# The second MLP product of five quads of token tiles as seven half-size products

## The chip, the cores and the metric

One NeuronCore of a Trainium2 chip runs the kernel in one launch. The metric is the device time in microseconds, smaller is better. Engines are named as in the profile: PE is TensorE (PEld its weight loads), DVE VectorE, ACT ScalarE, POOL GpSimd, SP SyncE, which here only starts transfers.

## The reference, cut to what matters

The inputs are float32: q, k, v of 4 batches, 8 heads, 768 tokens, 64 wide; the model width is 512, the hidden width 2048.

```python
scores = q @ k^T / 8, masked by blocks of 32        # per batch and head
x   = softmax(scores) @ v                            # -> batch, 768 tokens, 512
a1  = alpha1 * x + beta1
u   = x + lam * einsum('ts,bsd->btd', w_tok, a1)     # product over tokens
a2  = alpha2 * u + beta2
out = u + lam * (relu(a2 @ w_ch1) @ w_ch2)           # the MLP, per token
```

The change is in the last product, hidden (768 x 2048) times w_ch2 (2048 x 512), of two of the four batches. The kernel multiplies the columns of w_ch2 by lam beforehand (`w2b`).

## The kernel before

Heads go in pairs, 16 pairs in all, four to a batch. `emit_qk` (L582) makes the scores of a unit on TensorE, `emit_exp` (L600) their exponentials on ScalarE into an `eT` tile, `emit_keep` (L617) multiplies them by a mask on VectorE, and `emit_pv_keys` (L652) multiplies by v into the PSUM tile `op`, of which there is one. `emit_finish` (L669, L670) divides by the row sums into `x_sb`, and so frees `op` for the next head. `emit_a1pp` (L686, L687, mostly on POOL) makes a1. When two pairs are done, `job_tok2` (L826) makes the product over tokens for them in three groups; each is added to `x_sb` on VectorE (L838, an eviction) and cast to bf16 into `ubf` (`emit_cast`, L844).

The MLP needs u transposed. `emit_udma` (L868) lets a transposing DMA of the SP queue do this, and `emit_uscale` (L877) applies alpha2 and beta2. `job_ut` (L853, L854) does the same on TensorE and VectorE; it serves pairs 2 and 3 only. `job_f1(b, c, n)` (L891, L898) makes 128 hidden channels of 384 tokens: four matmuls of 384 columns and a ReLU on ScalarE into `hts`. There are 32 such jobs to a batch. `job_f2(b, o, g)` (L910) makes a quarter of the second product of a tile of 128 tokens: four matmuls of 512 columns, sixteen in all to a tile, in one PSUM bank; after the last, VectorE adds x (L919) into `ot`, which SP stores. The last tile of all goes in two column parts, 384 and 128 wide (`job_f2_cols`, L930, L938).

PSUM has eight banks: two `sp` tiles of two banks for the scores, three `mm` banks that go round, and one `op`.

The order is written by hand. The first five pairs run under a plan; the other eleven follow strings in which one letter is one job, in program order: q three units of scores, x an exponential, k a mask, p a pv job, f a `job_f1`, g a quarter of `job_f2`, T a third of `job_tok2`, d and v the DMA and the scaling of u, digits what the plan has for that time. `W1` takes nine rows to the end of batch 0's heads and beyond, `W2` twelve rows of three units, one batch, and runs twice (batch 2's and batch 3's heads, with the MLP of the batch before); `W3` is the last stage, the token product and MLP of batch 3:

```python
WEAVE = W1 + W2 * (B - 2) + W3
```

Every engine works through its own queue in that order; Tile's semaphores make an instruction wait for what it reads, and for the readers of what it overwrites. So an instruction that waits holds up all that stand behind it on its engine.

Of the kernel before, what the change touches and what calls it, by code (L numbers as in the profile page):

```python
# [25 lines left out]
DM = 512  # L26
P = 128
NT = S // P
NH = 4 * DM // P
QC = 384  # L30
NP = H // 2
# [11 lines left out]
W1 = [  # L43
# [9 lines left out]
]  # L53
W2 = [
# [12 lines left out]
]  # L67
W3 = [
# [3 lines left out]
]  # L72
WEAVE = W1 + W2 * (B - 2) + W3
ENG = {
    "kT0": 0,
    "kT1": 0,
# [153 lines left out]
def kernel(  # L230
# [16 lines left out]
    nc = tc.nc  # L247
# [22 lines left out]
    ap_ = ctx.enter_context(tc.tile_pool(name="attn", bufs=1))  # L270
# [4 lines left out]
    def ptile(shape, dt, name):  # L275
        return pp.tile(shape, dt, name=name, tag=name)
# [36 lines left out]
    qk0 = ap_.tile([P, 2, NT, 2, D], BF, name="qk", tag="qk", bufs=1)  # L313
# [9 lines left out]
    qTs = [ptile([P, 2, S], BF, f"qTs{i}") for i in range(NQB // 2)]  # L323
    kTs = [ptile([P, 2, S], BF, f"kTs{i}") for i in range(NQB // 2)]
# [24 lines left out]
    for n, src in enumerate((moe_lam, moe_alpha1, moe_beta1)):  # L349
# [10 lines left out]
        out=identb[:],  # L360
        in_=identb[:],
# [32 lines left out]
    for o in (slice(0, 4), slice(4, NT)):  # L394
# [47 lines left out]
    def sp_tile():  # L442
        return psum.tile([P, 2, 512], FP, name="sp", tag="sp", bufs=2)
# [111 lines left out]
    x_sbs = {}  # L555
# [137 lines left out]
    al2T, be2T = ab2T[:, 0:4], ab2T[:, 4:8]  # L693
# [97 lines left out]
    ubfs = {}  # L791
# [49 lines left out]

    def emit_cast(i, sl):
        b, hp = i // NP, i % NP
        nc.vector.tensor_copy(out=ubfs[i][:, sl, :], in_=x_sbs[b][:, sl, ts(hp, P)])  # L844

    def job_ut(i, half=None):
        b, hp = i // NP, i % NP
        if hp == 0:
            uTs[b] = ap_.tile([P, 4, S], BF, name="uT", tag="uT", bufs=2)
        sl = slice(0, NT) if half is None else slice(3 * half, 3 * half + 3)  # L850
        tps = mm_tile((P, NT, P), BF)
        for o in range(NT)[sl]:
            nc.tensor.transpose(tps[:, o, :], ubfs[i][:, o, :], identb[:])  # L853
        nc.vector.tensor_scalar(  # L854
            out=uTs[b][:, hp, :].rearrange("p (o t) -> p o t", o=NT)[:, sl, :],
            in0=tps[:, sl, :],
            scalar1=al2T[:, hp : hp + 1],
            scalar2=be2T[:, hp : hp + 1],
            op0=ALU.mult,
            op1=ALU.add,  # L860
        )


    uraws = {}
# [8 lines left out]
    def emit_uscale(i):  # L873
        b, hp = i // NP, i % NP
        if hp == 0:
            uTs[b] = ap_.tile([P, 4, S], BF, name="uT", tag="uT", bufs=2)
        nc.vector.tensor_scalar(  # L877
            out=uTs[b][:, hp, :],
            in0=uraws.pop(i)[:],
            scalar1=al2T[:, hp : hp + 1],  # L880
            scalar2=be2T[:, hp : hp + 1],
            op0=ALU.mult,
            op1=ALU.add,
        )

    def job_f1(b, c, n):
        if n == 0:
            hts[(b, c)] = ap_.tile([P, NH, QC], BF, name="hts", tag="hts", bufs=2)
        ps = mm_tile()
        for dk in range(4):  # L890
            nc.tensor.matmul(  # L891
                ps[:, 0:QC],
                w1b[:, dk, ts(n, P)],
                uTs[b][:, dk, ts(c, QC)],
                start=(dk == 0),
                stop=(dk == 3),
            )
        nc.scalar.activation(  # L898
            hts[(b, c)][:, n, :], ps[:, 0:QC], AF.Relu
        )  # L900

    chs = {}

    def job_f2(b, o, g):
        if g == 0:
            chs[(b, o)] = mm_tile()
        ps = chs[(b, o)]
        ht = hts[(b, o // 3)]
        for nk in range(4 * g, 4 * g + 4):
            nc.tensor.matmul(  # L910
                ps[:],
                ht[:, nk, ts(o % 3, P)],
                w2b[:, nk, :],
                start=(nk == 0),
                stop=(nk == NH - 1),
            )
        if g == 3:
            ot = ap_.tile([P, DM], FP, name="ot", tag="ot", bufs=3)
            nc.vector.tensor_tensor(  # L919
                out=ot[:], in0=x_sbs[b][:, o, :], in1=ps[:], op=ALU.add  # L920
            )
            nc.sync.dma_start(
                out[b].rearrange("(p o) n -> p o n", o=NT)[:, o, :], ot[:]
            )

    def job_f2_cols(b, o, sl):
        ps = mm_tile()
        ht = hts[(b, o // 3)]
        for nk in range(NH):
            nc.tensor.matmul(  # L930
                ps[:, sl],
                ht[:, nk, ts(o % 3, P)],
                w2b[:, nk, sl],
                start=(nk == 0),
                stop=(nk == NH - 1),
            )
        ot = ap_.tile([P, DM], FP, name="ot", tag="ot", bufs=3)
        nc.vector.tensor_tensor(  # L938
            out=ot[:, sl], in0=x_sbs[b][:, o, sl], in1=ps[:, sl], op=ALU.add
        )  # L940
        nc.sync.dma_start(
            out[b].rearrange("(p o) n -> p o n", o=NT)[:, o, sl], ot[:, sl]
        )

    NPAIR = B * NP
    WIDE = [
# [28 lines left out]
    ]  # L975
    N1 = MP * len(WIDE)
    LAG = 2
    todo = {"f": [], "g": [], "t": []}

    def start_mlp(b):  # L980
        todo["f"] += [
            lambda c=c, n=n: job_f1(b, c, n) for c in range(2) for n in range(NH)
        ]
        os_ = range(NT) if b < B - 1 else range(NT - 1)
        todo["g"] += [lambda o=o, g=g: job_f2(b, o, g) for o in os_ for g in range(4)]

    def start_pair(i):
        if i % 2 == 0:
# [152 lines left out]
    def token(t, p):  # L1141
        if t == "p":
            pv_next()
        elif t == "k":
            if kept:
                emit_keep(kept.pop(0))
        elif t in "012":
            fns(3 * p + int(t), False)
            fns(3 * p + int(t), True)
        elif t == "L":  # L1150
            if p // 3 + 2 < NPAIR:
                emit_load(p // 3 + 2)
        elif t in "QKY":
            if p // 3 + 1 < NPAIR:
                if t == "Y":
                    emit_lay(p // 3 + 1, "v")
                else:
                    emit_tdma(p // 3 + 1, t.lower())
        elif t == "q":
            for u in range(3 * p, 3 * p + 3):  # L1160
                emit_qk(u)
            exps.extend(range(3 * p, 3 * p + 3))
            exp_next()
        elif t == "x":
            exp_next()
        elif t == "s" and late:
            start_pair(late.pop(0))
        elif t == "T":
            todo["t"].pop(0)()
        elif todo.get(t):  # L1170
            todo[t].pop(0)()

    for p, text in enumerate(WEAVE):
        for t in text.replace(" ", ""):
            token(t, N1 // 3 + p)
    assert not (todo["f"] or todo["g"] or todo["t"] or pend or kept)
    for sl in (slice(0, 3 * P), slice(3 * P, DM)):
        job_f2_cols(B - 1, NT - 1, sl)
# [1 line left out]
_INS = ['q', 'k', 'v', 'sampled_blocks', 'moe_alpha1', 'moe_beta1', 'moe_w_tok', 'moe_alpha2', 'moe_beta2', 'moe_w_ch1', 'moe_w_ch2', 'moe_lam']  # L1180
_OUTS = [((4, 768, 512), 'float32')]
# [25 lines left out]
```

## Time and profile before

| | |
|---|---|
| timed runs | 302.43, 302.67, 302.77 us, median 302.67 |
| span of the profiled execution | 300.1 us (its own time is its span and some 2.6 us around it, by the median) |
| busy TensorE, VectorE, ScalarE, POOL | 293.2, 195.6, 212.7, 112.0 us |
| granted TensorE clock | 1.000 |
| start of batch 3's L891 stage | 255.49 us |
| end of TensorE's work | 297.07 us |

In the profile L12 is line 12 of the kernel, `out<-in` the tiles, and a figure such as 128x512 partitions by elements. Rows of the chain give start, length and what. Rows of the timeline give start, length from the first start to the last end, engine, line and operation, with the idle time before in brackets and who ended it. Rows of groups give the count, the busy time and the mean length of one. A matmul's own length is longer than its share of a stream, since they overlap in the array; so paces are taken from the chain.

### The profile page before, as it was taken

To read this page: it belongs to the slowest core of one execution; us is meant where nothing else is said; L and a number is where in the kernel's file an instruction comes from. 1 tells how busy PE (TensorE), PEld (TensorE's weight loads), DVE (VectorE), ACT (ScalarE), POOL (GpSimd) and SP (SyncE) were. 2 spreads that over 40 slices of the span, in tenths; PEclk is the share of its full clock that TensorE was granted. 3 is DMA by queue.
4 is the path that set the end of the run, shared out by engine and by line. 5 is a ranking of instruction groups with operands and counts; after the bars stand their busy time and mean duration, and the time that the engine had idled before them with its cause. 6 is when DMAs were issued, how large, how long until landed. Compare 5 with 4: busy or idle time off the path is not lost.

```text
span 300.1 us, 7192 instructions
## 1 busy us (share of the span) xinstructions
PE 293.2 (98%) x2970; PEld 183.2 (61%) x2995; DVE 195.6 (65%) x374; ACT 212.7 (71%) x314; POOL 112.0 (37%) x151
## 2 busy tenths in 40 slices
PE   7999999999999999999999999999999999999996
PEld 2788888664577565555675565565576564555543
DVE  4979899985688796963669687972769672000012
ACT  5999999998899944998878763998779400673210
POOL 8997887632525700564315320362322200000000
PEclk9999999999999999999999999999999999999999
DMA  6999999951491993629835693629102004000011
GB/s 182 187 201 187 189 166 196 194 94 28 101 171 21 142 178 81 131 46 149 127 57 86 110 176 85 120 64 135 49 18 52 37 35 122 37 0 37 35 70 70
DMA packets 57929, 31.26 MB, mean 104 GB/s; under 512 B 37989, under 2 KB 54673, under 8 KB 57897
## 3 DMA queue, kind: packets, MB, share of 16 engines
q0 software_dynamic: 16752, 14.22, 33.1%
q1 hardware_dynamic: 40820, 16.19, 26.3%
q8 instruction: 23, 0.38, 0.5%
q10 hardware_dynamic: 324, 0.40, 0.5%
q14 instruction: 10, 0.07, 0.1%
HBM read 29.75 MB, written 6.29 MB: 120 GB/s over the span
## 4 chain that ended last, share of the span: by engine, by line
PE 94%; ACT 3%; DMA 1%; issue 1%; DVE 0%; ACTq 0%
PE mm L891 28%; PE mm L910 26%; PE sp L582 10%; PE op L652 9%; PE mm L826 8%; PE mm L582 4%; PE mm L802 3%; ACT eT L600 2%; PE op L629 2%; PE mm L629 1%; PE mm L930 1%; DMA ms<-ms_c 1%; PE mm L780 1%; PE mm L492 1%; PE mm L532 0%
## 5 line engine op out<-in xcount | busy, mean ns | idle before, releaser
L600 ACT ACTIVATE eT<-sp,expb 128x1024 f16<-128x1024 f32 x111 | 118.3, 1121 | 1.8 <-PE sp L582 1.1
L891 PE MATMUL mm<-uT,w1b 128*128 128x384 bf16 x512 | 92.6, 326 | 0.1
L898 ACT ACTIVATE hts<-mm 128x384 bf16<-128x384 f32 x128 | 60.9, 500 | 42.1 <-PE mm L891 41.5
L617 DVE TENSOR_TENSOR eT<-eT,mask 128x1024 f16<-128x1024 f16 x99 | 80.2, 840 | 15.9 <-ACT eT L600 15.7
L910 PE MATMUL mm<-w2b,hts 128*128 128x512 bf16 x343 | 84.4, 379 | 1.3 <-issue 0.3
L686 POOL TENSOR_TENSOR a1pp<-x_sb,vbc 128x384 bf16<-128x384 f32 x26 | 29.7, 1141 | 124.2 <-DVE x_sb L670 94.7
L891 PEld LDWEIGHTS <-w1b 128*128 128x128 bf16 x512 | 48.2, 98 | 33.3 <-issue 2.1
L600 ACT ACTIVATE eT<-mm,expb 128x512 f16<-128x512 f32 x66 | 41.8, 685 | 27.2 <-PE mm L582 26.8
L910 PEld LDWEIGHTS <-hts 128*128 128x128 bf16 x368 | 33.7, 98 | 38.4 <-issue 4.7
L919 DVE TENSOR_TENSOR ot<-x_sb,mm 128x512 f32<-128x512 f32 x23 | 15.8, 686 | 49.2 <-PE mm L910 41.8
L652 PEld LDWEIGHTS <-eT 128*128 128x128 f16 x792 | 29.9, 98 | 8.3 <-issue 1.3
L652 PE MATMUL op<-vext,eT 128*128 128x65 f16 x792 | 32.1, 194 | 0.2
L687 POOL TENSOR_TENSOR a1pp<-a1pp,vbc 128x384 bf16<-128x384 bf16 x26 | 27.7, 1065 | 2.1
L582 PE MATMUL sp<-qTs,kTs 88*128 88x512 bf16 (+1 forms) x120 | 26.9, 326 | 1.3 <-ACT kTs L432 0.8
L826 PE MATMUL mm<-a1pp,wtokT 128*128 128x256 bf16 x216 | 25.9, 273 | 0.0
L826 PEld LDWEIGHTS <-wtokT 128*128 128x128 bf16 x216 | 20.6, 98 | 5.5 <-issue 2.5
L582 PE MATMUL sp<-qhT,khT 64*128 64x256 bf16 (+1 forms) x176 | 19.7, 322 | 0.0
L838 DVE TENSOR_TENSOR x_sb<-x_sb,mm 128x512 f32<-128x512 f32 x18 | 12.3, 686 | 10.2 <-PE mm L826 10.1
L582 PEld LDWEIGHTS <-khT 64*128 64x128 bf16 x264 | 10.5, 94 | 12.2 <-issue 8.6
L629 PEld LDWEIGHTS <-eT 128*128 128x128 f16 x360 | 14.9, 97 | 3.8 <-issue 0.3
L670 DVE TENSOR_TENSOR x_sb<-op,rcp 128x384 f32<-128x384 f32 x28 | 15.6, 558 | 1.0
L844 DVE CAST ubf<-x_sb 128x256 bf16<-128x256 f32 (+1 forms) x44 | 13.7, 346 | 0.9
(94 smaller groups left out, 221.8 us busy)
## 6 DMA issues: line engine op xcount, KB each, us to landing
out_dram<-ot SPq DMA_DIRECT2D x23, 256.0 KB
qpad<-in_q_dram POOLq DMA_DIRECT2D x15, 192.0 KB, 4.8
kr<-in_k_dram POOLq DMA_DIRECT2D x15, 192.0 KB, 5.5
vr<-in_v_dram POOLq DMA_DIRECT2D x15, 192.0 KB, 6.1
w1b<-in_moe_w_ch_dram POOLq DMA_DIRECT2D x4, 512.0 KB, 9.1
w2b<-in_moe_w_ch_dram POOLq DMA_DIRECT2D x4, 512.0 KB, 8.1
hts<-in_moe_w_tok_dram POOLq DMA_DIRECT2D x2, 576.0 KB, 9.7
x_sb<-in_k_dram ACTq DMA_DIRECT2D x2, 192.0 KB
```

Source lines behind the costliest of these rows:

```text
L582: nc.tensor.matmul(sp[jj][:, dst], lhsT, rhs, start=True, stop=True, skip_group_check=True,)
L600: nc.scalar.activation(dst, at, AF.Exp, bias=expb[:], scale=SCALE)
L617: nc.vector.tensor_mul(out=e, in0=e, in1=keep)
L629: nc.tensor.matmul(op[0][:, o, :], ets[u][:, jj, h * QB + n * P : h * QB + n * P + P], vexts[i % NVB][:, w, 2 * jp + jj, :], start=op[1] == 0,
L652: nc.tensor.matmul(op[0][:, o, :], ets[u][:, jj, h * QB + n * P : h * QB + n * P + P], vexts[i % NVB][:, w, 2 * jp + jj, :], start=op[1] == 0,
L686: eng.tensor_tensor(out=dst, in0=x_sbs[b][:, :, cols], in1=bc[0], op=ALU.mult)
L687: eng.tensor_tensor(out=dst, in0=dst, in1=bc[1], op=ALU.add)
L826: nc.tensor.matmul(ps[:, o], wtokT[:, os_, ts(2 * n + o, P)], a1pps[i][:, os_, :], start=(os_ == 0 and o == 0), stop=(os_ == NT - 1 and o ...
L891: nc.tensor.matmul(ps[:, 0:QC], w1b[:, dk, ts(n, P)], uTs[b][:, dk, ts(c, QC)], start=(dk == 0), stop=(dk == 3),)
L898: nc.scalar.activation(hts[(b, c)][:, n, :], ps[:, 0:QC], AF.Relu)
L910: nc.tensor.matmul(ps[:], ht[:, nk, ts(o % 3, P)], w2b[:, nk, :], start=(nk == 0), stop=(nk == NH - 1),)
L919: nc.vector.tensor_tensor(out=ot[:], in0=x_sbs[b][:, o, :], in1=ps[:], op=ALU.add)
```

## The change

A quad is two tiles of tokens, t and t + 3, with the hidden channels in two halves and the output columns in two halves: a 2 x 2 block product, eight half products before. Now seven, in the form of Strassen's scheme with fewest sums. With A11, A12 (tile t, first and second half of the channels), A21, A22 (tile t + 3) and the quarters B11 to B22 of `w2b`:

- weight sums, once for all quads, sixteen VectorE jobs (`job_t`, letter A, L972 of the changed kernel): T1 = B12 - B11, T2 = B22 - T1, T4 = B21 - T2, T3 = B22 - B12; they lie in tiles that earlier stages leave free, and a new small one
- activation sums, four to a quad (`job_s`, letter S, L1018): X1 = A21 + A22, X2 = X1 - A11, A21 becomes A11 - A21, A12 becomes A12 - X2
- products of eight matmuls of 256 columns each (`mul`, `job_p`, letter g): 1 = A11 B11, 2 = A12 B21, 3 = (A12 - X2) B22, 4 = A22 T4, 5 = X1 T1, 6 = X2 T2, 7 = (A11 - A21) T3
- running sums in PSUM and, after each product, an addition of the 256 or 2 x 256 columns to `x_sb` on VectorE (`plus`, L1054); the output is stored from `x_sb`, and `ot` is gone.

Batch 2 has tiles 1, 4 and 2, 5 as quads (tiles 0 and 3 stay whole), batch 3 all three. In batch 2 product 1 lies in an `mm` bank, product 2 is added to the same half bank, and 6 starts another; in batch 3 product 1 has an `sp` bank, to which 6 and 5 are added, and product 2 an `mm` bank of its own. The last product 3 of all goes in two parts of 128 columns.

The second `W2` becomes `W2L`, with the sixteen A spread over its first nine rows, two f earlier and the first three S at its end; `W3` is new. In batch 3 the f jobs take the channel halves by turns, so that S jobs on half the rows can go between them. The casts and scalings of batch 3's last u go to ScalarE, and of the last two, one is turned by TensorE (letter U, `job_ut`) and one by the DMA.

In program order, around the first products of batch 2: scores of three units, a mask, product 1 of the first quad, a mask, an f job, product 2, an f job, a mask, 24 L652, product 1 of the second quad, scores, product 2 of it, where VectorE has three activation sums of the first quad ahead of the next masks.

```diff
 W2L = [
+    "q 0 p p A g k x L x p f A k 1 K 2 k",
+    "q Q 0 A g x g f v v s T T x A k 1 k p p g g T g g Y d 2 k",
+    "q A g 0 k g d 1 2 p x A k g x k",
+    "q A 0 p k x v Q v 1 2 p k x g k g",
+    "q A 0 p 1 g x A k f K k x f p p k 2 f",
+    "q A k 0 f x f p s f f x 1 L p A k 2 f f f k Y f",
+    "q f L f 0 f A k 1 f Y x f p g x f p f g A k k 2",
+    "q x A k x k Q 0 g 1 s f f g p 2 p f f k p f",
+    "q A T 0 k f 1 x A k f T x f 2 p k K p f",
+    "q x 0 x T k 1 k f 2 k f Q f d p L",
+    "q x 0 x K k g d k s f g f 1 k p p g 2",
+    "q Y x x S S S k g k 0 1 k 2 p g v g v g",
+]
 W3 = [
-    "p p p f g s g T T T g g d d v g g g g g g v g g g f f f f",
-    "f f f f f f f f f f f",
-    "f f f f f f g g f g g f f f f g g g g f g g f f g f g f f g g g g g g g g g g g g",
+    "p p p g s g g T T T S S S d g g U g v S S g g g g g f f f f",
+    "f f f f f f f f f f f f",
+    "f f f f f f f f S S S f f S S S f f S S S f f f f",
+    "S S g S g S g g g S S g S g S g g g S S g S g g g g g S g g g g g",
 ]
-WEAVE = W1 + W2 * (B - 2) + W3
+WEAVE = W1 + W2 + W2L + W3
...
     def emit_cast(i, sl):
-        nc.vector.tensor_copy(out=ubfs[i][:, sl, :], in_=x_sbs[b][:, sl, ts(hp, P)])
+        copy = nc.scalar.copy if i >= NPAIR - 2 else nc.vector.tensor_copy
+        copy(out=ubfs[i][:, sl, :], in_=x_sbs[b][:, sl, ts(hp, P)])
...
+    def affine(i, dst, src):
...
+        if i >= NPAIR - NP:
+            nc.scalar.activation(dst, src, AF.Identity, bias=c, scale=a)
+        else:
+            nc.vector.tensor_scalar(
+                out=dst, in0=src, scalar1=a, scalar2=c, op0=ALU.mult, op1=ALU.add
+            )
...
+    def job_t(dst, a, b, n, k=2):
...
+        nc.vector.tensor_tensor(
+            out=b_rows(dst, n, k),
+            in0=b_rows(a, n, k),
+            in1=b_rows(b, n, k),
+            op=ALU.subtract,
+        )
...
+    def job_s(b, t, n, r=slice(0, HN)):
...
+        nc.vector.tensor_tensor(
+            out=a_of(b, t, dst, r), in0=a_of(b, t, a, r), in1=a_of(b, t, c, r), op=op
+        )
...
+        for r in range(HN):
+            nc.tensor.matmul(
+                ps,
+                a_of(b, t, a)[:, r],
+                b_rows(m, r)[:, 0, cols],
+                start=(start and r == 0),
+                stop=(r == HN - 1),
+                skip_group_check=True,
             )
...
+        if n == 1:
+            mul(b, t, 1, bk[0][:, lo], True)
+            if tail:
+                plus(x[:, t, lo], bk[0][:, lo])
+            else:
+                plus(x[:, t, hi], bk[0][:, lo])
+                plus(
+                    x[:, t + 3].rearrange("p (h c) -> p h c", h=2), twice(bk[0][:, lo])
+                )
+        elif n == 2:
+            ps = bk[1] if tail else bk[0]
+            mul(b, t, 2, ps[:, lo], tail)
...
+    REST = (6, 7, 5, 4, 3)
+    P_ORDER = {
+        2: [(0, g, "g") for g in range(4)]
+        + [(t, n) for t in (1, 2) for n in (1, 2)]
+        + [(3, g, "g") for g in range(4)]
+        + [(t, n) for t in (1, 2) for n in REST],
+        3: [(t, n) for t in range(2) for n in (1, 2)]
+        + [(t, n) for t in range(2) for n in REST]
+        + [(2, n) for n in (1, 2) + REST],
+    }
```

More of the change, by code (lines that the diff above doesn't have):

```diff
@@ L900, in job_f1 @@
         )
+        did.add(("f", b, c, n))
     chs = {}
@@ L917, in job_f2 @@
         if g == 3:
-            ot = ap_.tile([P, DM], FP, name="ot", tag="ot", bufs=3)
-            nc.vector.tensor_tensor(
-                out=ot[:], in0=x_sbs[b][:, o, :], in1=ps[:], op=ALU.add
-            )
[L922 to L943, printed above, removed]
+            x = x_sbs[b][:, o, :]
@@ new lines, with b_rows @@
+    tpool.append(tmore[:])
+    bq = {
+        (1, 1): (slice(0, HN), slice(0, HC)),
+        (1, 2): (slice(0, HN), slice(HC, DM)),
+        (2, 1): (slice(HN, NH), slice(0, HC)),
+        (2, 2): (slice(HN, NH), slice(HC, DM)),
+    }
+    def b_rows(name, n, k=1):
+        if name in bq:
+            rows, cols = bq[name]
+            return w2b[:, rows.start + n : rows.start + n + k, cols]
+        m = HN * ("T1", "T2", "T4", "T3").index(name) + n
+        assert m // 6 == (m + k - 1) // 6
+        return tpool[m // 6][:, m % 6 : m % 6 + k]
@@ new lines, with mul @@
+    PROD = {
+        1: ("11", (1, 1), 0),
+        2: ("12", (2, 1), 0),
+        3: ("12", (2, 2), 4),
+        4: ("22", "T4", 0),
+        5: ("X1", "T1", 1),
+        6: ("X2", "T2", 2),
+        7: ("21", "T3", 3),
+    }
+    banks = {}
+    def mul(b, t, n, ps, start, cols=slice(0, HC)):
+        a, m, need = PROD[n]
+        assert m in bq or all((m, r) in did for r in range(0, HN, 2))
+        if need:
+            assert all(("S", b, t, need, r) in did for r in range(HN))
+        c, half = {"1": (0, 0), "X": (1, 0)}.get(a[0], (1, 0))
+        if need == 0:
+            h, half = divmod(int(a) - 11, 10)
+            assert all(("f", b, h, HN * half + r) in did for r in range(HN))
+        for r in range(HN):
[6 more added lines that the diff above has]
+                skip_group_check=True,
+            )
```

154 lines of the change are left out of this document (131 added, 23 removed).

## The prediction, made before the changed kernel ran

> **What bounds the kernel now.** I read the page's busy times first, then its slices, then the chain of waits.
>
> ```profile
> PE 293.2 (98%) x2970; PEld 183.2 (61%) x2995; DVE 195.6 (65%) x374; ACT 212.7 (71%) x314; POOL 112.0 (37%) x151
> PE   7999999999999999999999999999999999999996
> DVE  4979899985688796963669687972769672000012
> POOL 8997887632525700564315320362322200000000
> PEclk9999999999999999999999999999999999999999
> PE 94%; ACT 3%; DMA 1%; issue 1%; DVE 0%; ACTq 0%
> ```
>
> TensorE (PE) works in every slice, its clock is granted in full, and 94% of the chain that ended last is TensorE itself. So a matmul taken away shortens the kernel, as long as TensorE then finds its next operand ready. VectorE (DVE) is free only in the last sixth of the span; before that it is nearly as full as TensorE. Three of the five quads lie in the free part, two and all the weight sums in the full part.
>
> The chain in order of time gives the pace of each kind of matmul (start, length, what):
>
> ```profile
> 242.07 3.93 PE mm L826 x36
> 255.49 13.65 PE mm L891 x84
> 279.95 1.73 PE mm L910 x8
> 293.56 3.51 PE mm L930 x32
> 297.09 0.29 DVE ot L938
> ```
>
> In a stream one matmul costs 1.73/8 = 0.216 us at 512 columns, 13.65/84 = 0.1625 us at 384, and 3.93/36 = 0.109 us at 256. TensorE ends at 297.07; the last sum, its store and the end of the program take the other 3.0 us of the span of 300.1 us. The median of the timed runs is 302.67 us, so 2.6 us lie around the span; I add differences to 302.67.
>
> **The change on TensorE.** Per quad, 32 matmuls of 512 columns (6.92 us) become 56 of 256 (6.11 us): 0.81 us saved, so 1.61 us for the two quads of batch 2 and 2.43 us for the three of batch 3. The end: L930's 32 matmuls are 16 of 384 columns (2.60 us) and 16 of 128, so the latter take 0.91 us, 0.057 each. The new last product is 16 of 128 columns too, where 8 of 256 would be 0.87, and the old split cost 0.05 over 16 whole ones: nothing either way. The turn of the last u adds six transposes.
>
> ```profile
> L853 PE MATMUL mm<-ident,ubf 128*128 128x128 bf16 x12 | 1.2, 219 | 0.0
> L826 PEld LDWEIGHTS <-wtokT 128*128 128x128 bf16 x216 | 20.6, 98 | 5.5 <-issue 2.5
> ```
>
> They cost from 6 x 0.057 = 0.34 us (streamed) to 6 x 0.219 = 1.3 us (not overlapped); I take 0.4, since they stand in a stream. TensorE's work falls by 1.61 + 2.43 - 0.4 = 3.6 us.
>
> More matmuls need more weight loads: one of 98 ns for each 109 ns, where there was one for 216. If none were hidden, 280 x 0.098 = 27 us; but L826 has just this ratio and runs 36 pairs in 3.93 us, so I charge nothing. The Trainium skill (TensorE: Matmul & The Clock Gate, Back-to-back issue gap) has a rule that speaks against the change: a real stream of loads and matmuls runs at about 131 ns per matmul at 512 columns and 81 at 128, so that halving the columns saves little. With 98 ns at 256 (an estimate, a straight line between that page's figures) a quad would go from 4.2 to 5.5 us, and the five would cost 6.5 us. The trace's 216 and 109 ns disagree with that rule; they agree with the page's other form, columns over 2.4 GHz plus 2.5 ns.
>
> **The change on VectorE, where TensorE must now wait.** Prices:
>
> ```profile
> L919 DVE TENSOR_TENSOR ot<-x_sb,mm 128x512 f32<-128x512 f32 x23 | 15.8, 686 | 49.2 <-PE mm L910 41.8 <-remote 5.4 <-PE mm L891 1.1
> L764 DVE TENSOR_TENSOR w2b<-w2b,lam_bcb x16: 411/418/1133, 49.4 to 72.8; 128x512 bf16<-128x512 bf16 x16
> L938 DVE TENSOR_TENSOR ot<-x_sb,mm 128x384 f32<-128x384 f32 x1 | 0.6, 553 | 1.9 <-PE mm L930 1.9
> L938 DVE TENSOR_TENSOR ot<-x_sb,mm 128x128 f32<-128x128 f32 x1 | 0.3, 289 | 0.3 <-PE mm L930 0.3
> 179.90 1.29 DVE L617 TENSOR_TENSOR eT<-eT,mask 128x1024 f16<-128x1024 f16 x2
> ```
>
> Two masks (L617) take 1.29 us in a row. Taking 0.69 for one, as for L919's like time, each holds the queue for 0.60 and its result shows 0.09 later. A sum of eight activation rows (128x1024, two bytes) has the form of a mask: 0.60. A weight sum (128x512, two bytes) is L764's form: 0.42, up to 1.13. Adding a 256-column product to x (a "read" below) lies between L938's 0.29 and 0.55: 0.42, or 0.33 in the queue; a 512-column one is L919's 0.69.
>
> (a) The sixteen weight sums.
>
> ```profile
> 164.00:186.90 22.90, 22.64 (x210) 12.94 (x211) 16.69 (x34) 12.79 (x18) 5.38 (x7) 1.00 0.67 122
> 186.90:199.40 12.50, 12.40 (x146) 7.12 (x145) 12.19 (x19) 11.61 (x17) 4.80 (x4) 1.00 0.57 111
> 199.40:227.70 28.30, 28.20 (x279) 18.05 (x280) 15.86 (x30) 23.72 (x41) 8.96 (x9) 1.00 0.31 54
> 198.94 0.56 DVE L670 TENSOR_TENSOR x_sb<-op,rcp 128x384 f32<-128x384 f32 x1
> 199.81 0.53 PE L652 MATMUL op<-vext,eT 128*128 128x65 f16 x12
> ```
>
> The columns after the length are TensorE, its loads, VectorE, ScalarE, POOL. In the first and third stretch VectorE has 6.2 and 12.4 us of idle time for eleven of the sums (4.6 us): nothing, or 0.42 each without that idle time. The sixth to the tenth stand in the second, where VectorE is busy 12.19 of 12.50 us. At its end the finish of a head (L669, L670) empties the only op bank, at 199.50, and TensorE's next L652, which writes that bank, starts at 199.81. So 5 x 0.42 = 2.1 us meet 0.31 + 0.31 us of slack: 1.5 us of waiting; with steps of 0.33 1.0. I take 1.3; up to 2.5 if the slow price falls on one or two, down to 0.
>
> (b) Products 1 and 2 of batch 2's first quad go in here:
>
> ```profile
> 228.09 0.43 PE sp L582 x6
> 231.01 0.65 PE mm L891 x4
> 228.12 1.27 ACT L600 ACTIVATE eT<-mm,expb 128x512 f16<-128x512 f32 x2
> 229.41 1.42 DVE L617 TENSOR_TENSOR eT<-eT,mask 128x1024 f16<-128x1024 f16 x1 [0.21 <-ACT eT L600]
> 229.28 1.00 POOL L686 TENSOR_TENSOR a1pp<-x_sb,vbc 128x384 bf16<-128x384 f32 x1 [9.22 <-DVE x_sb L670]
> ```
>
> Product 2 adds to product 1's half bank, so it waits until VectorE has read product 1, once 256 and once 2 x 256 columns. Both reads stand behind the mask that starts at 229.41, after the exponentials, and takes 1.42 with POOL beside it. They end at 229.41 + 1.33 + 0.33 + 0.69 = 231.8. TensorE ends the scores at 228.52, product 1 at 229.4 and the one L891 job between at 230.05: it waits 1.75 us, and the next scores' and heads' matmuls behind it. With a mask of 0.69, 1.0 us.
>
> (c), (d) The second quad, and the heads behind it:
>
> ```profile
> 233.26 0.32 PE mm L582 x4
> 233.58 0.43 PE sp L582 x4
> 236.50 0.36 PE op L652 x12
> 237.53 0.19 DVE L669 RECIPROCAL rcp<-op 128x6 f32<-128x6 f32 x1
> 237.76 0.56 DVE L670 TENSOR_TENSOR x_sb<-op,rcp 128x384 f32<-128x384 f32 x1
> 238.59 1.10 PE op L652 x36
> ```
>
> (c) The reads of its product 1 take 0.33 + 0.69 and TensorE has the eight score matmuls (0.75) between: 0.3 us. (d) From there VectorE has three activation sums (1.8), three masks (1.8), a read (0.33) and a finish (0.23 + 0.56): 4.7 us until the op bank is free. TensorE covers product 2 (0.87), twelve L652 (0.36) and twelve L910 (2.6): 3.8, so 0.9 us of waiting. Before, the finish ended at 238.32 and L652 followed at 238.59, with the same masks and no sums.
>
> (e) In the last stage product 7 of the second quad needs its activation sum. From the end of the third L826 group VectorE has that group's eviction (0.60 in the queue), three sums (1.8), reads of 0.60, 0.33 and 0.33, and the sum itself (0.69): 4.4 us. TensorE covers products 5, 4, the transposes, products 3 and 6: 4 x 0.87 + 0.4 = 3.9. Wait 0.5 us.
>
> What I charge at nothing:
>
> ```profile
> L310 ACT CAST qk<-x_sb 128x256 bf16<-128x256 f32 x1 | 0.4, 407 | 0.4 <-DMA x_sb<-in_k_dram 0.4
> 234.77 2.12 ACT L600 ACTIVATE eT<-sp,expb 128x1024 f16<-128x1024 f32 x2
> 247.08 1.22 SPq L868 DMA_TRANSPOSE uraw<-ubf  x1
> 249.83 0.48 DVE L877 TENSOR_SCALAR uT<-uraw,ab2T 128x768 bf16<-128x768 bf16 x1 [2.58 <-DMA uraw<-ubf]
> ```
>
> The moved casts come after ScalarE's last exponentials (234.77). An eviction (0.69) and two casts (0.8) stand before the last transposes, under products 5 and 4 (1.74): cover 0.2 us, and 0.4 lost per cast that is late. The other u still goes by SP's transposing DMA, 249.83 - 247.08 = 2.75 us, then a scaling; it has the second quad's five products (4.4 us). If that cover failed, 1 us. For batch 3 VectorE needs per quad four sums (2.7 with halves) and reads of 4 x 0.33 + 2 x 0.60, 5.2 us beside TensorE's 6.1, and between two products on one bank there stands another of 0.87 us: no wait; one failing cover per quad, 1 us. The last stores put 128 KB more behind TensorE's end: 0 to 0.3 us, I take 0.1.
>
> Sum: -3.6 + 1.3 + 1.75 + 0.3 + 0.9 + 0.5 + 0.1 = +1.25 us; 302.67 + 1.25 = **303.9 us**. Waits at their low ends (0 + 1.0 + 0 + 0.4 + 0.2) give -2.0, at their high ends (2.5 + 2.2 + 0.6 + 1.2 + 1.0, and 0.3) +4.2.
>
> **Rivals.** Faster: VectorE's queue keeps up and most of the 3.6 us comes through. It decides where the waits sum to under 3.0 us (then 302.1). For it: TensorE's work falls for sure, and few rows tell how VectorE's queue shifts against TensorE's. Against: (b) alone follows from one queue order and four rows. With (b) at 1.0, (c) and (d) at 0.3 and 0.4 and the rest hidden it gives 302.67 - 3.6 + 1.7 + 0.1 = 300.9. Chance 0.26. Even: waits of 3.0 to 4.1 us eat the gain, 302.1 to 303.2: 0.14. Slower still: the activation sums run at the slow price of the mask, 1.3 in the queue, so that in batch 3 four sums of 1.3 and reads of 2.5, 7.7 us, pass TensorE's 6.1: 3 x 1.6 more, 308.7. Against it: POOL, beside which the mask was slow, does nothing in the last slices. Chance 0.04. My forecast has the rest, 0.56, over 303.3 to 305.8.
>
> **How the numbers follow.** 0.2% is 0.6 us, about what a measurement of this kernel can tell from no change. Slower: 0.56 + 0.04 = 0.60; same 0.14; faster 0.26. The range, 301.2 to 305.8, leaves out the better half of the first rival, the last, and the forecast's far end.
>
> **What would show it.** Product matmuls at 0.109 us; TensorE idle before products 2 of batch 2 (1.75 and 0.3), before an L652 (0.9), before a product 7 (0.5), and 1.3 over the heads in the stretch of the fullest queue; batch 3's L891 stage starting 3.5 us after 255.49 (-1.6 + 0.4 + 4.75), and no idle time after it. I am wrong if the waits sum to under 3 us, or if the products of batch 3 have gaps.

## The result, and the profile after

The changed kernel took 303.68 us (median of six, 303.63 to 305.70) against 302.41 for the kernel before on the same chip: a ratio of 1.0053, interval 1.0031 to 1.0075, so 1.27 us slower where 1.25 was forecast. A second series gave 303.70 (four runs) against 302.09 (twenty-one): 1.0054, interval 1.0040 to 1.0068, or 1.61 us. The first profiled execution, the one of 305.70, had lost 1.6 us in the opening, which the change does not touch; so the profile read here is that of the second series, an execution of 303.72 us with a span of 302.0. Time and span are some 1.7 us apart in every run that lists both, not the 2.6 put around the span of the kernel before; so its profiled execution took some 301.8 us, and the two traces differ by more than the medians do.

Its page, where the page of before was shown: busy times, three slices, the chain by engine.

```profile
PE 292.4 (97%) x3113; PEld 194.3 (64%) x3113; DVE 219.9 (73%) x434; ACT 218.8 (72%) x324; POOL 111.2 (37%) x151
...
PE   7999999999999999999999999899998989999995
...
DVE  4978999985788797954577897993867778204674
...
PEclk9999999999999999999999999999999999999999
...
PE 87%; DVE 5%; POOL 3%; ACT 2%; issue 1%; POOLq 0%
```

VectorE has 24.3 us more, in its empty last sixth and also in the full part before it. TensorE, which was 9 in all but its first and last slice, now has three of 8, from 189, 227 and 242 us on, and the clock is granted as before. The chain that ended last goes through VectorE for 5%, where it was 0%.

TensorE's timeline from 186 us on has five waits and shows no other. They are those that the prediction named, but (a) stands 9 us earlier than it said, and before a matmul that waits for a mask instead of the op bank (start, length, what, and in brackets the idle time with who ended it):

```profile
188.89 0.54 PE L670 MATMUL op<-vext,eT 128*128 128x65 f16 x12
190.19 0.54 PE L670 MATMUL op<-vext,eT 128*128 128x65 f16 x12 [0.76 <-DVE eT L635]
...
231.90 0.81 PE L910 MATMUL mm<-uT,w1b 128*128 128x384 bf16 x4
234.30 1.03 PE L1044 MATMUL mm<-w2b,hts 128*128 128x256 bf16 x8 [1.58 <-DVE x_sb L1054]
...
238.70 1.03 PE L1044 MATMUL mm<-w2b,hts 128*128 128x256 bf16 x8 [0.35 <-DVE x_sb L1054]
...
239.93 2.75 PE L930 MATMUL mm<-w2b,hts 128*128 128x512 bf16 x12
243.47 1.28 PE L670 MATMUL op<-vext,eT 128*128 128x65 f16 x36 [0.78 <-DVE x_sb L688]
...
254.51 0.60 PE L1044 MATMUL sp<-kTs,xs 128*128 128x256 bf16 x4
255.85 0.83 PE L1044 MATMUL mm<-qk,hts 128*128 128x256 bf16 x6 [0.74 <-DVE hts L1018]
```

These are (a), (b), (c), (d), (e) in this order. The idle time in brackets is less than what the wait costs. A matmul's own length runs past the start of the next one, so the delay has to be counted from start to start. For (b): the L910 job before it starts at 231.90 and is worth 0.65 us of stream (4 x 0.1625), so product 2 could have started at 232.55 and started 1.75 later; the bracket says 1.58. In the same way (a) is 190.19 - (188.89 + 0.36) = 0.94, (c) 0.52 (the last scores start at 237.75 and take 0.43), (d) 243.47 - (239.93 + 12 x 0.216) = 0.95, and (e) 255.85 - (254.51 + 4 x 0.109) = 0.90. The brackets are 0.16 to 0.18 short each time.

The chain, from the end of the second quad on, answers to the rows 255.49 to 297.09 of before:

```profile
259.56 20.80 PE mm L910 x128
280.36 0.87 PE sp L1044 x8
281.23 0.87 PE mm L1044 x8
...
297.06 1.32 PE mm L1044 x16
298.38 0.46 PE op L1044 x8
298.84 0.02 issue
298.86 0.29 DVE x_sb L1054
```

Eight matmuls of 256 columns take 0.87 us, 0.109 each, in every product, with no gap from 259.56 to 298.84: 39.28 us, where the kernel before took 41.58 from 255.49 to 297.07. The last stage gained 2.30 us, and the stages before it lost 4.07, where 3.5 was forecast. Of the 4.07, 0.16 was there before the first weight sum at 171.3 us: an exponential that starts at 160.73 in the kernel before starts at 160.89 here.

### The profile page after: what moved, and what is told of

Its sections match the earlier page's. It is cut to its first block, busy times and chain, and to the rows that moved or that the text cites. A ratio compares the mean times of both kernels' runs of the same rounds, so it can differ in the third digit from the quotient of the medians.

```text
span 304.0 us, 7518 instructions
## 1 busy us (share of the span) xinstructions
PE 292.7 (96%) x3113; PEld 194.1 (64%) x3113; DVE 220.4 (72%) x434; ACT 218.8 (72%) x324; POOL 111.5 (37%) x151
## 4 chain that ended last, share of the span: by engine, by line
PE 79%; DVE 9%; DMA 6%; ACT 2%; POOL 2%; issue 1%; SPq 0%; POOLq 0%
PE mm L910 25%; PE mm L930 14%; PE sp L600 8%; PE mm L844 7%; PE op L670 7%; PE mm L1044 5%; PE sp L1044 3%; DMA qpad<-in_q_dram 3%; PE mm L600 3%; DVE eT L635 2%; DMA uraw<-ubf 2%; ACT eT L618 2%; PE op L647 2%; PE mm L820 1%; DVE x_sb L1054 1%
## 5 line engine op out<-in xcount | busy, mean ns | idle before, releaser
L910 PE MATMUL mm<-uT,w1b 128*128 128x384 bf16 x512 | 91.6, 326 | 0.0
L704 POOL TENSOR_TENSOR a1pp<-x_sb,vbc 128x384 bf16<-128x384 f32 x26 | 28.7, 1105 | 131.8 <-DVE x_sb L688 96.9
L910 PEld LDWEIGHTS <-w1b 128*128 128x128 bf16 x512 | 48.1, 98 | 31.8 <-issue 2.1
L930 PE MATMUL mm<-w2b,hts 128*128 128x512 bf16 x224 | 54.7, 379 | 0.0
L670 PEld LDWEIGHTS <-eT 128*128 128x128 f16 x792 | 29.8, 98 | 10.9 <-DVE x_sb L688 2.3
L670 PE MATMUL op<-vext,eT 128*128 128x65 f16 x792 | 32.3, 194 | 1.8 <-DVE x_sb L688 0.8
L930 PEld LDWEIGHTS <-hts 128*128 128x128 bf16 x224 | 19.7, 97 | 22.4 <-issue 3.9
L705 POOL TENSOR_TENSOR a1pp<-a1pp,vbc 128x384 bf16<-128x384 bf16 x26 | 27.8, 1068 | 2.1
L844 PE MATMUL mm<-a1pp,wtokT 128*128 128x256 bf16 x216 | 25.9, 273 | 0.0
L844 PEld LDWEIGHTS <-wtokT 128*128 128x128 bf16 x216 | 20.7, 98 | 5.3 <-issue 1.8
L1044 PEld LDWEIGHTS <-hts 128*128 128x128 bf16 x208 | 19.5, 98 | 6.3 <-issue 2.9
L1018 DVE TENSOR_TENSOR xs<-hts 128x512 bf16<-128x512 bf16 (+1 forms) x8 | 3.7, 486 | 17.8 <-ACT hts L917 17.8
```

Source lines behind the costliest of these rows:

```text
L670: nc.tensor.matmul(op[0][:, o, :], ets[u][:, jj, h * QB + n * P : h * QB + n * P + P], vexts[i % NVB][:, w, 2 * jp + jj, :], start=op[1] == 0,
L704: eng.tensor_tensor(out=dst, in0=x_sbs[b][:, :, cols], in1=bc[0], op=ALU.mult)
L705: eng.tensor_tensor(out=dst, in0=dst, in1=bc[1], op=ALU.add)
L844: nc.tensor.matmul(ps[:, o], wtokT[:, os_, ts(2 * n + o, P)], a1pps[i][:, os_, :], start=(os_ == 0 and o == 0), stop=(os_ == NT - 1 and o ...
L910: nc.tensor.matmul(ps[:, 0:QC], w1b[:, dk, ts(n, P)], uTs[b][:, dk, ts(c, QC)], start=(dk == 0), stop=(dk == 3),)
L930: nc.tensor.matmul(ps[:], ht[:, nk, ts(o % 3, P)], w2b[:, nk, :], start=(nk == 0), stop=(nk == NH - 1),)
```

## The experiments

Theory: TensorE's work fell as counted, and VectorE's queue, by its order, gave back more in five waits in batch 2's part. Rivals: the smaller matmuls gain less than counted; or VectorE is simply full there, and a wait that is taken away comes back at the next place. All orders below are rows of the hand-written sequence; unless it is said otherwise the edit is made in the changed kernel (303.70). Every time is a median, with the interval of its ratio to the kernel before on the same chip. That kernel took 302.07 to 302.09 us on the chip of most of these runs, and 302.28 and 302.32 on two others, which four runs used (302.79, 299.97, 300.91 and 300.06); a difference between chips is uncertain by at least 0.2 us.

### Each wait by itself

**(b): the reads of product 1 ahead of the mask.**

```diff
-    "q x 0 x K k g d k s f g f 1 k p p g 2",
+    "q x 0 x K g k d k s f g f 1 k p p g 2",
```

> Wait (b). The first product of batch 2's first quad, and with it VectorE's two reads of it, is put ahead of the mask in program order; TensorE's order stays. Queue theory: the reads end at about 1.0 us after product 1 instead of 2.4, the L891-type job covers 0.65 of that, so the wait of 1.6 us falls to about 0.45 and the time by 1.1, to 302.5 us. Rival, VectorE is simply full and a wait moves when its work is moved: the mask comes 1 us later, the pv matmuls wait for it instead, and the time stays at 303.6.

Measured 302.55 (1.0006 to 1.0024): 1.15 less. The mask and reads in VectorE's timeline, first of the changed kernel, then with the edit:

```profile
231.91 1.41 DVE L635 TENSOR_TENSOR eT<-eT,mask 128x1024 f16<-128x1024 f16 x1 [0.22 <-ACT eT L618]
233.24 1.00 DVE L1054 TENSOR_TENSOR x_sb<-x_sb,mm 128x256 f32<-128x256 f32 x2
```

```profile
232.13 1.02 DVE L1054 TENSOR_TENSOR x_sb<-x_sb,mm 128x256 f32<-128x256 f32 x2 [0.41 <-PE mm L1044]
233.06 1.87 DVE L635 TENSOR_TENSOR eT<-eT,mask 128x1024 f16<-128x1024 f16 x2
```

Product 1 starts at 231.02 and 231.04, the reads 1.11 us earlier; the idle time before product 2 falls from 1.58 to 0.46, and the mask that now comes later is waited for by nobody. The wait was the queue's order.

**(a): five weight sums out of the fullest stretch**, put some rows later:

```diff
-    "q A g 0 k g d 1 2 p x A k g x k",
-    "q A 0 p k x v Q v 1 2 p k x g k g",
-    "q A 0 p 1 g x A k f K k x f p p k 2 f",
-    "q A k 0 f x f p s f f x 1 L p A k 2 f f f k Y f",
-    "q f L f 0 f A k 1 f Y x f p g x f p f g A k k 2",
-    "q x A k x k Q 0 g 1 s f f g p 2 p f f k p f",
-    "q A T 0 k f 1 x A k f T x f 2 p k K p f",
+    "q A g 0 k g d 1 2 p x k g x k",
+    "q 0 p k x v Q v 1 2 p k x g k g",
+    "q 0 p 1 g x k f K k x f p p k 2 f",
+    "q k 0 f x f p s f f x 1 L p A A k 2 f f f k Y f",
+    "q A f L f 0 f A k 1 f Y x f p A g x f p f g A k k 2",
+    "q x A k x k Q 0 g 1 s f f A g p 2 p f f k p f",
+    "q A T 0 k f 1 x A k f T x f 2 p A k K p f",
```

> Wait (a). The five weight sums in the fullest stretch go to the rows after it, where VectorE had idle time before; nothing else moves. Queue theory: the waits between 188 and 204 us go, 1.3 to 1.5 us, to 302.2 us. Rival, they cost nothing there, or cost as much in the later rows: 303.6.

Measured 302.77 (1.0016 to 1.0034): 0.93 less; the wait of 0.76 before the L670 at 190.19 is gone. The expectation went by the first execution's 1.5 us; in the second series' profile the exponentials had fallen 1.0 us behind those of the kernel before between 190 and 206 us, and with the edit 0.2. The term is about 1.0, and nearly all of it came back.

**(d): the three activation sums behind the finish of the head.**

```diff
-    "q Y x x S S S k g k 0 1 k 2 p g v g v g",
+    "q Y x x k g k 0 1 k 2 p S S S g v g v g",
```

> Wait (d). The three activation sums ahead of the last masks go behind the finish of the head. Queue theory: the op bank is free 1.8 us earlier, the wait of 0.8 us before the last 36 pv matmuls goes, and products 6 and 7 still find their sums: 302.9 us. Rival, the wait moves to product 6, which then waits for its sum: 303.6.

Measured 304.55 (1.0071 to 1.0102): 0.85 slower, the rival's figure and more. The wait for the op bank is gone; two others came. From the timelines of VectorE, POOL and TensorE with this edit:

```profile
243.55 0.68 DVE L1018 TENSOR_TENSOR xs<-hts 128x1024 bf16<-128x1024 bf16 x1
244.27 1.37 DVE L1018 TENSOR_TENSOR xs<-xs,hts 128x1024 bf16<-128x1024 bf16 x1
245.56 1.40 DVE L1018 TENSOR_TENSOR hts<-hts 128x1024 bf16<-128x1024 bf16 x1
...
248.28 0.56 DVE L705 TENSOR_TENSOR a1pp<-a1pp,vbc 128x384 bf16<-128x384 bf16 x1
```

```profile
243.71 1.38 POOL L704 TENSOR_TENSOR a1pp<-x_sb,vbc 128x384 bf16<-128x384 f32 x1 [8.63 <-DVE x_sb L688]
245.17 1.24 POOL L705 TENSOR_TENSOR a1pp<-a1pp,vbc 128x384 bf16<-128x384 bf16 x1
```

```profile
247.01 0.83 PE L1044 MATMUL mm<-qk,hts 128*128 128x256 bf16 x6 [0.27 <-DVE hts L1018]
...
248.90 4.10 PE L844 MATMUL mm<-a1pp,wtokT 128*128 128x256 bf16 x36 [0.84 <-DVE a1pp L705]
```

The finish releases POOL, whose two steps for the next head run from 243.71 to 246.41; the sums now stand beside them and take 1.37 and 1.40 instead of 0.68. Behind them the last head's finish and its a1pp on VectorE come late, and with them the token mixing. From the head's L670 ahead of it to that stage TensorE needs 8.35 us (240.55 to 248.90), and 7.62 without the edit (239.57 to 247.19): +0.73 of the 0.85 measured. The Trainium skill (SBUF — State Buffer, Who interferes with whom) has VectorE and GpSimd share one pair of ports under an exclusive lock, and a VectorE instruction with two SBUF inputs contend there with a GpSimd one that reads SBUF; the doubled sums and the longer POOL step (1.38, where its like took 1.00) agree.

**(d) again, two of the three sums put earlier**, where VectorE stood still for 1.24 us:

```diff
-    "q x 0 x K k g d k s f g f 1 k p p g 2",
-    "q Y x x S S S k g k 0 1 k 2 p g v g v g",
+    "q x 0 x K k g d k s f g f 1 k S S p p g 2",
+    "q Y x x S k g k 0 1 k 2 p g v g v g",
```

> The changed kernel, with the first two of the second batch-2 quad's... three activation sums that stand between product 2 and the masks put two steps earlier, into 1.24 us in which VectorE's queue stood still waiting for a product (the idle time before the reads at 237.63); the third sum stays. Theory, it is the queue order: the three sums before the finish cost (d), 0.78 us of TensorE waiting for the op bank, so this gives 303.7 - 0.78 = 302.9, and the step after it keeps its pace, because no two-byte sum lies beside GpSimd's two instructions on the next a1pp. Rival, the sums' work itself is too much for VectorE in this stretch wherever it stands (what putting them behind the finish could also mean, which gave 304.6): 303.7 or more. Second rival: the reads of the second quad's product 1 come later for the sums ahead of them, and (c) grows from 0.35 by what (d) loses: 303.5.

Measured 303.02 (1.0013 to 1.0037): 0.68 less. The wait for the op bank is gone and (c) grew, as the second rival had it, but only from 0.35 to 0.59: 0.95 - 0.24 = 0.71. So (d) was order too, and by these rows the loss of the edit before it came from the neighbour, not from the wrong wait.

**(e): product 7's sum ahead of the transposing DMA.**

```diff
-    "p p p g s g g T T T S S S d g g U g v S S g g g g g f f f f",
+    "p p p g s g g T T T S S S S d g g U g v S g g g g g f f f f",
```

> The changed kernel, with the one activation sum that product 7 of the second batch-2 quad needs moved up in the last stage's first row, ahead of the transposing DMA's issue and products 5, 4 and 3 of the first quad. Queue theory: TensorE's wait (e) of 0.74 us goes, and nothing else changes, since the first matmul of batch 3's L910 stage had its u 1.6 us before it: 303.7 - 0.7 = 303.0. Rival, the sum moved up delays the evictions and reads now behind it by 0.6 us and TensorE waits there, at the last six transposes: 303.5 to 303.9.

Measured 303.87 (1.0042 to 1.0080): nothing gained, as the rival said, at another place than it said. TensorE and VectorE:

```profile
255.41 0.82 PE L1044 MATMUL mm<-qk,hts 128*128 128x256 bf16 x6
...
257.25 1.03 PE L1044 MATMUL sp<-qTs,xs 128*128 128x256 bf16 x8 [0.80 <-DVE x_sb L1054]
```

```profile
251.78 0.69 DVE L856 TENSOR_TENSOR x_sb<-x_sb,mm 128x512 f32<-128x512 f32 x1 [0.62 <-PE mm L844]
...
256.18 0.68 DVE L1018 TENSOR_TENSOR hts<-hts,xs 128x1024 bf16<-128x1024 bf16 x1
256.78 0.41 DVE L1054 TENSOR_TENSOR x_sb<-x_sb,sp 128x256 f32<-128x256 f32 x1
```

Product 7 waits no more, but product 5 adds to the bank of product 6, and the read of that bank stands behind the last sum. From 251.78 to 257.19 VectorE never stands still; whichever of these instructions comes last is waited for.

**(e) again, two sums out of that stretch**, into the idle time between the evictions before it (0.76, 0.55, 0.62):

```diff
-    "p p p g s g g T T T S S S d g g U g v S S g g g g g f f f f",
+    "p p p g s g g T S T S T S S d g g U g v S g g g g g f f f f",
```

> The changed kernel, with three activation sums of batch 2 moved from behind the third eviction of the last token-mixing stage (L844) to behind its first and its second, where VectorE stood still for 0.76, 0.55 and 0.62 us; of the five sums one is then left behind the transposes. Moving product 7's sum alone had gained nothing: the wait of 0.74 before product 7 went, and one of 0.80 before product 5 came, for the read of product 6, which was now behind that sum. Theory, in the 5 us from the last eviction to that read VectorE never stands still, so only sums taken out of these 5 us help: two sums of 0.6 go, product 7 and product 5 both find their operand, 303.7 - 0.74 = 303.0. Rival, the sums between the evictions make these late, TensorE waits for a bank or ScalarE's casts for the last transposes: 303.7 or more.

Measured 302.79 (1.0010 to 1.0028): 0.91 less, with 0.90 from start to start. The trace, which does not depend on the chip's median, has batch 3's L910 stage start 11.26 us after the L844 stage (247.28 to 258.54), where it was 12.21 (247.19 to 259.40): 0.95 less. TensorE has no wait left from 247 us to the end of its work.

### All together

All four orders at once, with the version of (e) that gains nothing:

> All four changes of order together: the two reads ahead of the mask, five weight sums 4 to 7 us later, two activation sums in the gap, and product 7's sum early. Nothing is left out and no work is added or taken away, only VectorE's order changes. Theory, the waits (a), (b), (d), (e) are separate, so they add: 303.7 - 0.9 - 1.15 - 0.78 - 0.7 = 300.2, which would be 1.9 under the kernel before; what is left of waits is (c) 0.35, some 0.45 of (b) and 0.25 of (a), and the rest is the 3.6 us of TensorE work less these and some 0.6 not accounted for. Rival, VectorE is simply full in these stages, and a wait that goes comes back at the next place: 301.5 to 302.5.

Measured 301.25 (0.9956 to 0.9980): 2.45 less than the changed kernel, where the four single edits sum to 1.15 + 0.93 + 0.68 - 0.17 = 2.59. They add; what was missing to the 300.2 expected was (e), and (c), which had grown to 0.95 with two sums ahead of the reads. With one sum ahead, and (e) as in the last edit:

```diff
-    "q x 0 x K k g d k s f g f 1 k p p g 2",
-    "q Y x x S S S k g k 0 1 k 2 p g v g v g",
+    "q x 0 x K g k d k s f g f 1 k S p p g 2",
+    "q Y x x S S k g k 0 1 k 2 p g v g v g",
```

> All changes of order together (reads ahead of the mask, five weight sums later, one activation sum in the gap and two behind it, three among the evictions of the last L844 stage); all five quads with seven products, nothing left out. The version with product 7's sum moved and two sums in the gap took 301.25 and had waits of 0.95 before the second quad's product 2, and 0.80 before product 5. Theory: the second wait goes (0.75) and the first falls by 0.6 as one sum less is ahead of the reads, while the finish of the head has 0.4 us of slack for it: 301.25 - 0.75 - 0.4 = 300.1. Rival, VectorE is the bound in these stages and the waits come back: 301.2.

Measured **299.97** (0.9914 to 0.9939): 2.3 us faster than the kernel before and some 3.7 than the changed one, with the same work on every engine. TensorE's two remaining waits on VectorE:

```profile
232.15 1.03 PE L1044 MATMUL mm<-w2b,hts 128*128 128x256 bf16 x8 [0.46 <-DVE x_sb L1054]
...
236.55 1.03 PE L1044 MATMUL mm<-w2b,hts 128*128 128x256 bf16 x8 [0.35 <-DVE x_sb L1054]
```

A last edit put other matmuls of TensorE ahead of these two:

```diff
-    "q x 0 x K g k d k s f g f 1 k S p p g 2",
+    "q x 0 x K g k d k s f f g 1 k S p g p 2",
```

> The version with all changes of order (299.97), with TensorE's own order changed at the two places where it still waits for reads of VectorE: the second of the two L910 jobs goes from behind product 2 to ahead of it (0.65 us, for a wait of 0.46), and product 1 of the second quad goes ahead of a head's twelve L670 instead of behind them (0.37 us, for a wait of 0.35). VectorE's order stays but for that. Nothing left out. Theory, a wait for a read is covered just as well by other matmuls as by an earlier read: 299.97 - 0.46 - 0.35 = 299.2. Rival, the second L910 job takes a third of the three mm banks while ScalarE is behind its exponentials until 232.7, and a later matmul waits for that bank: 300.0 or more.

Measured 300.06 (0.9916 to 0.9943): no gain, and not for the rival's reason. The first wait went, and the second one grew:

```profile
232.29 1.04 PE L1044 MATMUL mm<-w2b,hts 128*128 128x256 bf16 x8
...
236.53 1.03 PE L1044 MATMUL mm<-w2b,hts 128*128 128x256 bf16 x8 [0.84 <-DVE x_sb L1054]
```

Product 2 of the second quad starts at 236.53, where it started at 236.55. It waits for VectorE, which goes without a pause from the reads of the first quad's product 1 to the finish of the head, from 231.07 to 240.54 before this edit and from 231.19 to 240.52 with it; the L670 that needs this finish starts at 240.59 and 240.57. So TensorE's own order is without effect there, and over these 9 us "VectorE is full" is right.

### The last batch alone, and the weight sums alone

Seven products in batch 3 only, batch 2 as before, the weight sums in batch 3's L910 stage:

```diff
-W2L = [
...
+W2L = W2
 W3 = [
-    "p p p g s g g T T T S S S d g g U g v S S g g g g g f f f f",
-    "f f f f f f f f f f f f",
-    "f f f f f f f f S S S f f S S S f f S S S f f f f",
+    "p p p f g s g T T T g g d d v g g g g g g v g g g f f f f",
+    "f A f A f A f A f A f A f A f A f A f A f A f A",
+    "f A f A f A f A f f f f S S S f f S S S f f S S S f f f f",
...
-STR = (2, 3)
+STR = (3,)
```

> Seven half-size products only for the three quads of the last batch; batch 2's two quads as 64 whole matmuls as before; the sixteen weight sums no longer among the masks of batch 2 but in the last batch's L910 stage, where VectorE has nothing else; the last u by its transposing DMA as before. Nothing is left out. Theory (the gain is TensorE's work and the loss is VectorE's queue in batch 2): no wait is added, and three quads give 3 x 0.81 = 2.4 us: 302.1 - 2.4 = 299.7, with an error of 0.3. Rival, the gain is not in the smaller matmuls as counted (a load for each 109 ns matmul): 301 to 302. Rival two: the weight sums delay the activation sums and product 1 of the last batch: 300.5.

Measured **299.84** (0.9907 to 0.9931): 2.23 faster than the kernel before. The casts and scalings of batch 3's last u stay on ScalarE here. Its exponentials run 0.3 us behind those of that kernel at 161 us, from the opening on, and 0.4 at 211. This kernel is as fast as the one with five quads in their best order (299.97): there batch 2's two quads save 1.61 us, and TensorE still gives back 0.63 and 0.52 before their products 2, 0.22 before the L670 at 240.59 and 0.34 for the transposes, 1.71 in all. So the quads of batch 2 showed no gain in any order tried.

VectorE's rows in batch 3's L910 stage (L897 in this kernel) show the price of a weight sum that nothing disturbs, four in 1.42 us, a step of 0.33:

```profile
255.90 0.69 DVE L926 TENSOR_TENSOR x_sb<-x_sb,mm 128x512 f32<-128x512 f32 x1 [2.77 <-PE mm L917]
256.50 1.42 DVE L959 TENSOR_TENSOR qTs<-w2b 128x512 bf16<-128x512 bf16 x4
...
261.52 0.42 DVE L959 TENSOR_TENSOR tmore<-w2b 128x512 bf16<-128x512 bf16 x1
```

The same with the sixteen sums back among batch 2's masks (A where the changed kernel has it, the two rows of f above undone):

> The kernel with seven products in the last batch only (299.84), with the sixteen weight sums put back to the places that they have in the changed kernel, among the masks and heads of batch 2. Nothing left out. It measures part (a) by itself. Theory: the sums cost the 1.1 us by which the changed kernel's exponentials fell behind the former kernel's between 190 and 205 us, and nothing elsewhere: 300.9. Rival, the sums have slack once batch 2 has no other new work: 299.9. What is then left between this and the changed kernel's 303.7, 2.8 us by the theory, is batch 2's two quads: -1.2 of TensorE's work, +3.45 of waits (b) to (e), and 0.55 that no wait in the list carries.

Measured 300.91 (0.9942 to 0.9969): 1.07 for (a) by itself. The 2.79 us from here to 303.70 are batch 2's two quads: (b) to (e) and the transposes make 4.45 from start to start, so -1.66 is left for the quads' matmuls, by difference, where -1.61 was counted.

## Why the prediction was right, and where a step was off

The sign was as forecast, the mechanism too but for (a), and the time to within 0.4 us. That the first series met 1.25 with 1.27 is partly luck: the terms were off by up to 0.4, mostly towards a longer time, and the second series gave 1.61. Term by term, in us, by start-to-start delays:

| step | predicted | measured |
|---|---|---|
| batch 3's three quads | -2.43 | -2.30 in the trace; -2.23 alone |
| batch 2's two quads | -1.61 | -1.66, by difference only |
| six transposes of u | +0.4 | +0.33 (252.87 to 253.20) |
| (a) weight sums | +1.3 | +1.07 alone |
| (b) read of product 1 behind the mask | +1.75 | +1.75 |
| (c) second quad's product 2 | +0.3 | +0.52 |
| (d) op bank behind three sums | +0.9 | +0.95 |
| (e) product 7's sum | +0.5 | +0.90 |
| last stores | +0.1 | +0.20 (from the last sum to the end of the span, 2.67 and 2.87) |

With -2.30 and -1.61 the measured column gives +1.81, where the two series gave +1.27 and +1.61; the two traces differ by 1.9 in their spans (302.0 and 300.1), 0.16 of it from before the first weight sum.

**TensorE's work.** 0.109 us per 256-column matmul held in every product of batch 3, with a load for each. The rule that spoke against it (the Trainium skill, TensorE: Matmul & The Clock Gate, Back-to-back issue gap) would, by the prediction's estimate from it, have made each quad 1.3 us longer; the three of batch 3, run alone, made the kernel 2.23 us faster.

**(b)**, the largest term, came out exactly, from one order and four rows: the mask of 1.41 beside POOL, then two reads. The prediction also had right who waits: the edit that swapped these two gave 1.15 back.

**(c) and (e)** were undersized, and both for the same 0.2 us: a product's read starts that long after its last matmul's share of the stream is over, and the prediction set VectorE's and TensorE's times against each other as if they began together. For (c) product 1's stream ends at 236.55 + 0.87 = 237.42, and its reads start at 237.63; they take 1.02, as predicted, against 0.75 of cover. For (e) the last L844 group's stream ends at 251.12, its eviction starts at 251.32, and from there VectorE needs 4.47 (4.4 predicted) against 3.83 of cover (3.9). The prediction also took VectorE's queue only as far as product 7's sum. It goes on without a pause to the read that product 5 needs, 5.4 us in all, so that moving the sum within it gained nothing (303.87) and only taking work out of it helped (302.79).

**(a)** was 1.07 for 1.3, at another place: not a head's matmul waiting for the op bank at 199.5, but one at 190.19 waiting for a mask. In the kernel before, the first mask behind a finish starts 0.24 us ahead of POOL's next a1pp and takes 0.68, and it is POOL that takes longer. With the changed kernel a weight sum stands ahead of that mask, which so starts 0.10 behind POOL and takes 1.49, to 190.13. First the kernel before, then the changed one:

```profile
188.16 0.68 DVE L617 TENSOR_TENSOR eT<-eT,mask 128x1024 f16<-128x1024 f16 x1
188.40 1.30 POOL L686 TENSOR_TENSOR a1pp<-x_sb,vbc 128x384 bf16<-128x384 f32 x1 [14.27 <-PE mm L582]
```

```profile
188.32 0.41 DVE L972 TENSOR_TENSOR qTs<-w2b,qTs 128x512 bf16<-128x512 bf16 x1
188.55 1.03 POOL L704 TENSOR_TENSOR a1pp<-x_sb,vbc 128x384 bf16<-128x384 f32 x1 [14.24 <-PE mm L600]
188.65 2.81 DVE L635 TENSOR_TENSOR eT<-eT,mask 128x1024 f16<-128x1024 f16 x2
```

So a sum that holds the queue for 0.33 us made the matmul wait 0.94. With the weight sums later the mask starts ahead of POOL again (188.23 and 188.47) and takes 0.68. The prediction's slack at the op bank was not what counted, and that its 1.3 came near 1.07 is luck. The rest of the 1.07 is in no wait that the profile lists, and stays open.

**At nothing** stood the load per matmul, the batch 3 tail (5.2 us of VectorE beside 6.1), the casts and the scaling on ScalarE and the other u's DMA. None of them shows a wait. The moved f jobs, not charged either, only change the order.

**The rivals.** "VectorE keeps up" failed by 5 us of waits. The orders above make the kernel 2.3 faster than before, more than the rival's 1.8, so most of the loss was a matter of order. Not all of it was: over the 9 us around batch 2's first four half products VectorE is full, and its two quads show no gain in the best order either. The masks' slow price did not reach batch 3, where POOL does nothing.

## What to carry to other kernels

Work that is traded from the bounding engine to a second one pays only where the second one has idle time at that place: three quads gave 2.2 us in a stage with an idle VectorE (299.84); two more, and the weight sums, beside a full queue cost 3.9 (303.70), and 0.1 in the best order tried (299.97). So try the idle place alone first. Then read the second engine's queue instruction by instruction: move the read that frees a bank ahead of work nobody waits for yet, and fill its idle gaps; if a moved instruction only changes who waits, the stretch is full, and work has to leave it. Look also at what runs beside the new place, not only at whether it is free.

## What the runs showed of the hardware that was not expected

The idle time that the profile shows before a matmul was 0.16 to 0.18 us less than the delay from start to start, in each of five waits; where an edit took such a wait away whole, the trace behind it moved by the delay and not by the bracket (0.95 us earlier, where the delay was 0.90 and the bracket 0.74).

Beside POOL's L704 and L705, a 128x1024 sum or mask of two SBUF operands took mostly 1.37 to 1.49 instead of 0.68. They did not run at one slower pace: from 150 us on in four traces (before, changed, the sums behind the finish, the best order) all 43 that started during a step of POOL ended 0.55 us after that step, whatever they took themselves (0.96 to 1.49). Masks ended at 190.13 and 191.46 behind steps that ended at 189.59 and 190.91, the sums at 245.64 and 246.96 behind 245.09 and 246.41. Where VectorE started first it kept its 0.68, and POOL's step took 1.30 (188.40) or 1.38 (243.71) instead of 1.00. So in these rows it counts which of the two starts first, and 0.1 us decided it in wait (a). But the reads that add a PSUM operand kept their price: 1.02 us for two at 232.13 while POOL's step ran from 231.79:

```profile
231.79 1.00 POOL L704 TENSOR_TENSOR a1pp<-x_sb,vbc 128x384 bf16<-128x384 f32 x1 [10.47 <-DVE x_sb L688]
```

So the reads were not only earlier ahead of the mask but also the better neighbour for POOL.
